# Query loads in whole-row lines, with part of the turned queries moved between partition groups by ScalarE and VectorE, in a pooled attention kernel with a routed feed-forward layer

## The chip, the cores and the metric

The kernel runs on one NeuronCore of one Trainium2 chip. The metric is the device time of one execution in microseconds; an execution's time is compared as the median of several runs, and one execution was profiled.

## The reference

Queries, keys and values come as `(8, 8, 1152, 64)` float32: eight batches, eight heads, 1152 rows, 64 features. Neighbouring query rows are averaged in twos, so 576 pooled queries meet 1152 keys. The attention output of a batch, its heads side by side, is `x` with 576 tokens of 512 features. A gate ranks the tokens of each batch; the 128 best go through a two-layer feed-forward network and are added back.

```python
q_pool = q.reshape(B, H, S // 2, 2, D).mean(axis=3)
scores = np.matmul(q_pool, k.transpose(0, 1, 3, 2)) / np.sqrt(D)
attn = softmax(scores)                      # over the 1152 keys
x = np.matmul(attn, v)                      # bridged to (B, 576, 512)
s = np.einsum('bsd,d->bs', x, w_gate)
top = the 128 largest of s[b]
out[b] = x[b]
out[b, top] = x[b, top] + sigmoid(s[b, top]) * (relu(x[b, top] @ w1) @ w2)
```

## The kernel before

**Order.** The class `_Plain` writes every engine's order out by hand: each engine runs its instructions in the order in which `run` issues them. Two heads make a pair (`hp`), four pairs a batch, 32 pairs in all. The 576 pooled queries of a pair are taken in two halves of 288, `s = 0` and `s = 1`, so `run` loops over 64 halves `h`. One half issues, in this order, the loads of a later pair and stores (at `s = 1`), the scores of this half, small copies of sums of an earlier pair, the row sums of this half's exponents (`folded`), work of earlier halves, `prepare_pair` for the next pair (at `s = 0`), and the product with the values for the half before (`weighted`).

**Layout.** Queries and keys have to stand with their features on the partitions: head 0 of the pair on partitions 0 to 63, head 1 on 64 to 127. VectorE's transpose turns blocks of 32x32, each within its own group of 32 partitions. So `load_pair` puts the first 32 features of head 0 on partition group 0, the last 32 on group 1, and head 1 in the same way on groups 2 and 3 (`quarters`). Each line that such a load reads is 32 floats, 128 bytes. `load_pair` issues four loads for `kb` (L742) and four for `qb` (L745) on SP's queue; the values `v_sb` come by L756, outputs leave by L1024, on the same queue.

**Steps of a pair.** `prepare_pair` adds the two query rows of each pooled query on GpSimd (`qp`, L767), and VectorE turns keys into `kT` (L770) and queries into `qT` (L774). `scores` makes nine PSUM tiles per half with 36 matmuls of 64x64 by 288 columns (L869): the features of one head are the contraction, the columns are 288 queries of `qT`. ScalarE takes the exponent of each tile (L876). `folded` adds the exponents up: GpSimd adds two thirds of them (`acc`, L908), VectorE folds the last third and then `acc` (L913, twice) and finishes with a short reduction (L923). `weighted` multiplies the exponents of the half before with the values (L887, 36 matmuls); ScalarE copies the result out of PSUM (`two`, L895), GpSimd adds its halves (L897), VectorE turns it (`avb`, L966). The rest of a pair is the gate product (L976, L1035), the sums spread over the partitions (L938, L944, L953), their reciprocals (L1005) and the division (L1013).

**Routing.** After the fourth pair of a batch the generator `routed` ranks its tokens in pieces that `units("mid")`, `units("sums")` and `units("end")` put between the steps of later halves. On VectorE these are comparisons (L1145, L1154, L1164), searches (L1229) that wait for a line loaded through DRAM (`lines`, L1198), and a transpose of the gathered tokens (L1284). The feed-forward layers run on TensorE (L1437, L1312, L1332) and, for the first six batches, two batches at a time, with sums on VectorE (L1450) and GpSimd (L1403).

**Buffers.** `qb` and `qp` have one buffer each, `kb`, `kT`, `qT` and `v_sb` two. PSUM holds four tiles of two banks, which scores, `weighted` and the feed-forward layers share.

Of the kernel before, what the change touches and what calls it, by code (L numbers as in the profile page):

```python
# [10 lines left out]
P = 128  # L11
BLK = 32

G = 3
F32 = mybir.dt.float32
# [12 lines left out]
def _any_scores(  # L28
# [450 lines left out]
    pairs = [(b, hp) for b in range(B) for hp in range(NPAIR)]  # L479
    in_pair = [(j, t) for j in range(2) for t in range(NF)] + [(0, NF)]  # L480
    upcoming = load_pair(*pairs[0])
    run(prepare_pair(upcoming))
    preparing = iter(())
    routing = iter(())
# [23 lines left out]
    for n, (b, hp) in enumerate(pairs):  # L508
        pair = upcoming
        run(preparing)  # L510
        if hp == 0:
            x = xpool.tile([P, NT, Dm], F32, name="x")
        for i, (j, t) in enumerate(in_pair):
            now = {"pair": pair, "j": j, "t": t, "x": x}
            advance(now)
            if two is not None and two["t"] == NF and two["pair"]["hp"] == NPAIR - 1:
                run(routing)
                routing = routed(two["pair"]["b"], two["x"])
            one, two = now, one
            if i == 0 and n + 1 < len(pairs):  # L520
                upcoming = load_pair(*pairs[n + 1])
                preparing = prepare_pair(upcoming)
            if n == 0 and i == 0:
                load_weights()
            if i >= 3:
                next(preparing, None)
            next(routing, None)
# [7 lines left out]
class _Plain:  # L535
# [199 lines left out]
    def load_pair(self, b, hp):  # L735

        nc = self.nc
        kb = self.load.tile([P, self.KB, BLK], F32, name="kb")
        qb = self.load.tile([P, self.QB, 2, BLK], F32, name="qb", bufs=1)
        for j, ds, rows in self.quarters():  # L740
            of = self.k[b, 2 * hp + j, :, ds]
            nc.sync.dma_start(kb[rows, :, :], of.rearrange("(i n) d -> i n d", i=BLK))  # L742
        for j, ds, rows in self.quarters():
            of = self.q[b, 2 * hp + j, :, ds].rearrange("(i m) d -> i m d", i=BLK)
            nc.sync.dma_start(qb[rows, :, :, :].rearrange("i n r d -> i (n r) d"), of)  # L745
        return {"k": kb, "q": qb, "b": b, "hp": hp}

    def load_values(self, pair):
# [12 lines left out]
    def prepare_pair(self, pair):  # L761

        nc = self.nc
        qp = self.load.tile([P, self.QB, BLK], F32, name="qp", bufs=1)
        kT = pair["kT"] = self.load.tile([P, self.S], F32, name="kT")
        qT = pair["qT"] = self.load.tile([P, self.Sp], F32, name="qT")
        nc.gpsimd.tensor_tensor(  # L767
            out=qp[:, :, :], in0=pair["q"][:, :, 0, :], in1=pair["q"][:, :, 1, :], op=ALU.add
        )
        nc.vector.transpose(  # L770
            kT.rearrange("p (c g i) -> p c g i", c=self.NC, i=BLK),
            pair["k"].rearrange("p (g c) d -> p c g d", c=self.NC),
        )
        nc.vector.transpose(qT[:, :], qp.rearrange("p n d -> p (n d)"))  # L774

    def load_first(self, b, hp):

# [784 lines left out]
    def run(self):  # L1562
        nc = self.nc
        pairs = [(b, hp) for b in range(self.B) for hp in range(self.NPAIR)]
        n_halves = 2 * len(pairs)
        halves = []
        self.routing, self.waiting = [], set()
        upcoming = self.load_first(*pairs[0])
        self.first_constants()
        self.prepare_first(upcoming)  # L1570
        self.constants()
        loaded = self.load_pair(*pairs[1]) if len(pairs) > 1 else None
        self.load_gate()
        weights = self.weight_loads()
        sums = self.weight_sums() if self.paired else iter(())
        for h in range(n_halves):
            n, s = divmod(h, 2)
            if s == 0:
                pair = upcoming
                if pair["hp"] == 0:  # L1580
                    part = self.ffn.tile([P, self.NPAIR, self.QB], F32, name="part")
                pair["part"] = part
            else:
                loaded = None
                if n + 2 < len(pairs):
                    loaded = self.load_pair(*pairs[n + 2])
                if n + 1 < len(pairs):
                    self.load_values(upcoming)
                if n > 1:
                    self.stored(halves[h - 4]["pair"])  # L1590
            if h > 1:
                next(weights, None)

            if 5 < h < 14 or 18 < h < 23:
                for _ in range(2 - s):
                    next(sums, None)
            half = {"pair": pair, "s": s}
            halves.append(half)
            self.scores(half)
            if h > 1:  # L1600

                of = halves[h - 2 - s]["pair"]
                if s == 0:
                    of["groups"] = self.side_by_side(of["sum"].rearrange("p j n -> p (j n)"))
                else:
                    self.spread(of)
            self.units("mid")
            if h > 2:
                self.gated(halves[h - 3])
            self.folded(half)  # L1610
            if h > 2:
                self.scored(halves[h - 3])
            self.units("sums")
            if h > 1:
                self.multiplied(halves[h - 2])
            if h > 1 and s == 0:
                last = halves[h - 1]["pair"]
                last["total"] = self.added(last["groups"])
            if s == 0 and loaded:
                upcoming = loaded  # L1620
                self.prepare_pair(upcoming)
            if h > 0:
                self.weighted(halves[h - 1])
                self.drained(halves[h - 1])
            if h > 2 and s == 1:
                self.normalized(halves[h - 2]["pair"])
            if h > 3 and s == 0:

                self.divided(halves[h - 3]["pair"])
            self.units("end")  # L1630
        for _ in weights:
            pass
        for _ in sums:
            pass

        def pieces(unit, n=None):
            for i, _ in enumerate(unit):
                if i + 1 == n:
                    break


        left = [unit for _, unit, _ in self.routing]
        old = left.pop() if left else iter(())
        older = left.pop() if left else iter(())
        assert not left
        self.gated(halves[-3])
        pieces(old, 1)
        self.weighted(halves[-1])
        self.drained(halves[-1])
        self.multiplied(halves[-2])  # L1650
        self.multiplied(halves[-1])
        self.scored(halves[-3])
        self.gated(halves[-2])
        pieces(older, 1)
        self.normalized(halves[-1]["pair"])
        self.gated(halves[-1])
        self.scored(halves[-1])
        _, new, _ = self.routing.pop()

        pieces(new, 1)  # L1660
        pieces(old, 1)
        for half in (halves[-3], halves[-1]):
            self.divided(half["pair"])
            self.stored(half["pair"])
        pieces(older, 2)
        pieces(new, 1)
        pieces(old, 1)
        pieces(older, 1)
        pieces(new, 3)
        pieces(older, 4)  # L1670
        pieces(old, self.NFC // 2)
        pieces(new, 1)
        low = self.counted()
        pieces(old, self.NFC // 2 + 1)
        pieces(older)
        pieces(new, 2)
        pieces(old)
        count = self.outside(low)
        pieces(new, 10)
        found = nc.values_load(count[0:1, 0:1])  # L1680
        E = mybir.EngineType
        self.tc.mark_branch_hint_location("again", found, [E.PE, E.DVE, E.Pool, E.Activation, E.SP])
        pieces(new)
        return found
# [61 lines left out]
```

## Time and profile before

| | |
|---|---|
| Median of 3 runs | 689.82 us (689.19 to 692.28) |
| The profiled execution | 689.66 us, its span 687.9 us |
| Busy: TensorE, weight load | 678.0 us (99%), 564.4 us (82%) |
| Busy: VectorE, ScalarE, GpSimd | 536.4 us (78%), 457.7 us (67%), 512.9 us (75%) |
| Granted TensorE clock, mean | 0.998 |
| DMA packets | 397059, of them 377232 under 512 bytes; 101.22 MB |
| Query loads `qb` | 124 issues of 144.0 KB, 3.7 us to landing |

The span goes from the first to the last instruction; the execution's own time has a little around it. Busy shares are of the span. A group of instructions is named by its line, engine, operation and tiles (out<-in). The time behind the last bar of a group is idle time of the engine just before it, with what ended it. In a timeline a row gives start, length, engine, line, operation, tiles and count, and in square brackets the idle time before it.

### The profile page before, as it was taken

To read this page: it belongs to the slowest core of one execution; us is meant where nothing else is said; L and a number is where in the kernel's file an instruction comes from. 1 tells how busy PE (TensorE), PEld (TensorE's weight loads), DVE (VectorE), ACT (ScalarE), POOL (GpSimd) and SP (SyncE) were. 2 spreads that over 40 slices of the span, in tenths; PEclk is the share of its full clock that TensorE was granted. 3 is DMA by queue.
4 is the path that set the end of the run, shared out by engine and by line. 5 is a ranking of instruction groups with operands and counts; after the bars stand their busy time and mean duration, and the time that the engine had idled before them with its cause. 6 is when DMAs were issued, how large, how long until landed. Compare 5 with 4: busy or idle time off the path is not lost.

```text
span 687.9 us, 23660 instructions
## 1 busy us (share of the span) xinstructions
PE 678.0 (99%) x9972; PEld 564.4 (82%) x9972; DVE 536.4 (78%) x842; ACT 457.7 (67%) x998; POOL 512.9 (75%) x503
## 2 busy tenths in 40 slices
PE   9999999999999999999999999999999999999996
PEld 6668899989997998786888899777788899867776
DVE  3867888998999796786698977695879989688930
ACT  5677777777777783847777677583877777575220
POOL 4788888798887775867996978483999888569241
PEclk9999999999999999999999999999999999999999
DMA  9888878688779767953878787783777777644311
GB/s 173 158 176 182 209 143 202 130 155 165 138 167 171 159 136 140 229 101 80 227 129 176 135 166 148 139 197 64 158 190 171 140 152 163 118 116 118 81 47 36
DMA packets 397059, 101.22 MB, mean 147 GB/s; under 512 B 377232, under 2 KB 381200, under 8 KB 395664
## 3 DMA queue, kind: packets, MB, share of 16 engines
q1 hardware_dynamic: 395408, 95.13, 67.1%
q0 software_dynamic: 1296, 4.20, 1.9%
q8 instruction: 80, 1.31, 0.8%
q10 hardware_dynamic: 240, 0.30, 0.2%
q14 instruction: 35, 0.29, 0.1%
HBM read 81.97 MB, written 17.62 MB: 145 GB/s over the span
## 4 chain that ended last, share of the span: by engine, by line
PE 83%; DVE 4%; DMA 4%; issue 4%; POOL 3%; ACT 1%; SPq 0%; POOLq 0%; DVEq 0%; ACTq 0%
PE ps L887 36%; PE ps L869 36%; PE ps L1437 8%; DVE fold L913 2%; DMA out_dram<-xe,index 1%; PE ps L1312 1%; POOL acc L908 1%; ACT p L876 1%; DMA v_sb<-in_v_dram 1%; DMA lines<-row_rank 1%; PE ps L616 1%; DMA row_rank<-both 0%; POOL prod L976 0%; POOL s L1403 0%; DVE pick L1164 0%
## 5 line engine op out<-in xcount | busy, mean ns | idle before, releaser
L876 ACT ACTIVATE p<-ps 128x576 f32<-128x576 f32 x576 | 320.4, 699 | 2.4 <-PE ps L869 2.4
L887 PE MATMUL ps<-p,v_sb 64*64 64x288 f32 x4608 | 296.7, 403 | 2.0 <-DMA v_sb<-in_v_dram 2.0
L869 PE MATMUL ps<-qT,kT 64*64 64x288 f32 x4608 | 296.4, 403 | 0.7 <-DVE token L637 0.5
L908 POOL TENSOR_TENSOR acc<-p 128x576 f32<-128x576 f32 x192 | 272.0, 1444 | 26.7 <-ACT p L876 26.1
L887 PEld LDWEIGHTS ps<-p,v_sb 64*64 64x64 f32 x4608 | 233.7, 133 | 49.9 <-ACT p L876 13.3
L869 PEld LDWEIGHTS ps<-qT,kT 64*64 64x64 f32 x4608 | 229.3, 133 | 51.4 <-ACT p L876 4.6
L913 DVE TRANSPOSE_TENSOR_REDUCE fold<-p 128x54 f32<-128x1728 f32 x64 | 126.0, 1968 | 32.8 <-ACT p L876 32.8
L913 DVE TRANSPOSE_TENSOR_REDUCE fold<-acc 128x54 f32<-128x1728 f32 x64 | 124.7, 1948 | 27.3 <-POOL acc L908 27.3
L895 ACT COPY two<-ps 128x576 f32<-128x576 f32 x64 | 40.8, 637 | 139.0 <-PE ps L887 131.6
L897 POOL TENSOR_TENSOR av<-two 128x288 f32<-128x288 f32 x64 | 51.2, 800 | 68.7 <-ACT two L895 65.4
L767 POOL TENSOR_TENSOR qp<-qb 128x576 f32<-128x576 f32 x31 | 43.7, 1409 | 14.0 <-DMA qb<-in_q_dram 12.9
L976 POOL TENSOR_TENSOR prod<-avb,w_gate 128x288 f32<-128x288 f32 x64 | 51.7, 808 | 1.5 <-DVE red L1035 1.3
L966 DVE STREAM_TRANSPOSE avb<-av 128x288 f32<-128x288 f32 x64 | 29.0, 453 | 23.2 <-POOL av L897 22.8
L770 DVE STREAM_TRANSPOSE kT<-kb 128x1152 f32<-128x1152 f32 x31 | 42.1, 1357 | 0.0
L953 ACT ACTIVATE sums<-total,tiny 32x18 f32<-32x18 f32 x124 | 38.2, 308 | 2.3 <-DVE total L944 0.3
L1013 POOL TENSOR_TENSOR x<-avb,rec 128x576 f32<-128x576 f32 x30 | 34.8, 1160 | 0.0
L1164 DVE SCALAR_TENSOR_TENSOR pick<-sc_row,gate_sc,before 128x128 f32<-128x128 f32 (+1 forms) x40 | 31.3, 782 | 1.4
L938 ACT COPY groups<-sum 32x36 f32<-32x36 f32 x124 | 27.3, 220 | 2.4 <-DVE sum L923 0.7
L1035 DVE TENSOR_REDUCE red<-prod 128x9 f32<-128x288 f32 x64 | 27.7, 433 | 0.1
L1445 ACT COPY s<-ps 128x256 f32<-128x256 f32 (+1 forms) x27 | 11.4, 447 | 20.8 <-PE ps L1437 20.8
L774 DVE STREAM_TRANSPOSE qT<-qp 128x576 f32<-128x576 f32 x31 | 22.6, 730 | 2.1 <-POOL qp L767 2.0
L923 DVE TENSOR_REDUCE sum<-fold 128x18 f32<-128x108 f32 x64 | 21.9, 342 | 2.2
(136 smaller groups left out, 481.7 us busy)
## 6 DMA issues: line engine op xcount, KB each, us to landing
kb<-in_k_dram SPq DMA_DIRECT2D x124, 144.0 KB, 4.5
qb<-in_q_dram SPq DMA_DIRECT2D x124, 144.0 KB, 3.7
v_sb<-in_v_dram SPq DMA_DIRECT2D x124, 144.0 KB, 3.5
tw<-tw SPq DMA_DIRECT2D x10, 1024.0 KB, 7.0
out_dram<-x SPq DMA_DIRECT2D x128, 72.0 KB, 3.0
lines<-row_rank SPq DMA_DIRECT2D x7, 640.0 KB, 4.6
w<-in_moe_w_dram SPq DMA_DIRECT2D x8, 512.0 KB, 6.3
tw<-tw SPq DMA_DIRECT2D x8, 512.0 KB, 5.6
```

What stands on the lines that cost most here:

```text
L767: nc.gpsimd.tensor_tensor(out=qp[:, :, :], in0=pair["q"][:, :, 0, :], in1=pair["q"][:, :, 1, :], op=ALU.add)
L770: nc.vector.transpose(kT.rearrange("p (c g i) -> p c g i", c=self.NC, i=BLK), pair["k"].rearrange("p (g c) d -> p c g d", c=self.NC),)
L869: nc.tensor.matmul(sc[keys, j, 0:n], lhsT=pair["kT"][rows, c * P + keys.start : c * P + keys.stop], rhs=pair["qT"][rows, qs], start=True, ...
L876: nc.scalar.activation(p[:, c // G, c % G, :, :], sc[:, :, 0:n], AF.Exp, scale=self.scale)
L887: nc.tensor.matmul(av[j * self.D : (j + 1) * self.D, e, 0:n], lhsT=half["pair"]["v"][keys, j, c, :], rhs=half["p"][keys, c // G, c % G, j, :],
L895: nc.scalar.copy(two[:, :, :], av[:, :, 0:n])
L897: nc.gpsimd.tensor_tensor(out=half["av"][:, :], in0=two[:, 0, :], in1=two[:, 1, :], op=ALU.add)
L908: nc.gpsimd.tensor_tensor(out=acc[:, u, :], in0=units[:, 0, u, :], in1=units[:, 1, u, :], op=ALU.add)
L913: nc.vector.tensor_reduce(fold[:, a, :], of.rearrange("p u (m d) -> p (u m) d", d=BLK), AX.X, ALU.add, apply_transpose=True,)
L953: self.nc.scalar.activation(tot[rows, :], pair["total"][:, j * self.QB : (j + 1) * self.QB], AF.Identity, bias=self.tiny[0:BLK, 0:1],)
L976: self.nc.gpsimd.tensor_tensor(out=pair["prod"][:, ns, :], in0=pair["avb"][:, ns, :], in1=self.w_gate[:, hp : hp + 1, :].broadcast_to([P, ...
L1437: nc.tensor.matmul(args[0], lhsT=args[1], rhs=args[2], start=k == 0, stop=k == n - 1)
```

## The change

`load_pair` no longer splits the queries by features. It reads 18 whole rows of 64 features, which lie one behind the other in DRAM, as one line of 4608 bytes: partition group 0 gets the first half's queries of head 0 (all 64 features), group 1 the second half's, groups 2 and 3 the same for head 1. The GpSimd addition stays, on tiles of another shape.

The turning now takes two transposes in `prepare_pair`, one for each 32 features. Of these, two blocks per head stand where they belong: features 0 to 31 of the first half, and features 32 to 63 of the second half. The two others have to move between partition groups. `copied_across` copies features 0 to 31 of the second half from the upper to the lower group of the head, on ScalarE, one copy per head. `turned_across` then transposes features 32 to 63 of the first half once more from `qp` in the lower group, straight into the upper group, on VectorE, one transpose per head. Both are issued in the second half (`s == 1`) of the pair before the one whose queries they move: the copies after `spread`, the transposes after `folded`, `scored` and `units("sums")`. The first pair of the kernel is loaded in another way (`load_first`) and isn't touched, so 31 pairs are.

```diff
 def load_pair(self, b, hp):
-        qb = self.load.tile([P, self.QB, 2, BLK], F32, name="qb", bufs=1)
+        qb = self.load.tile([P, self.HB, 2, self.D], F32, name="qb", bufs=1)
...
-        for j, ds, rows in self.quarters():
-            of = self.q[b, 2 * hp + j, :, ds].rearrange("(i m) d -> i m d", i=BLK)
-            nc.sync.dma_start(qb[rows, :, :, :].rearrange("i n r d -> i (n r) d"), of)
+        of = self.q[b, 2 * hp : 2 * hp + 2].rearrange("j (i s m) d -> j s i (m d)", i=BLK, s=2)
+        for g in range(P // BLK):
+            rows = slice(g * BLK, (g + 1) * BLK)
+            nc.sync.dma_start(qb[rows, :, :, :].rearrange("i n r d -> i (n r d)"), of[g // 2, g % 2])
...
 def prepare_pair(self, pair):
-        qp = self.load.tile([P, self.QB, BLK], F32, name="qp", bufs=1)
+        qp = pair["turn"] = self.load.tile([P, self.HB, self.D], F32, name="qp", bufs=1)
...
-        nc.vector.transpose(qT[:, :], qp.rearrange("p n d -> p (n d)"))
+        for e in range(2):
+            nc.vector.transpose(qT[:, self.half_of(e)], qp[:, :, e * BLK : (e + 1) * BLK])
+
+    def half_of(self, s):
+        return slice(s * self.HALF, (s + 1) * self.HALF)
+
+    def crossing(self, j):
+        return slice(j * self.D, j * self.D + BLK), slice(j * self.D + BLK, (j + 1) * self.D)
+
+    def copied_across(self, pair):
+        qT = pair["qT"]
+        for j in range(2):
+            low, high = self.crossing(j)
+            self.nc.scalar.copy(qT[low, self.half_of(1)], qT[high, self.half_of(0)])
+
+    def turned_across(self, pair):
+        qp = pair.pop("turn")
+        for j in range(2):
+            low, high = self.crossing(j)
+            self.nc.vector.transpose(pair["qT"][high, self.half_of(0)], qp[low, :, BLK:])
...
 def run(self):
                     self.spread(of)
+            if s == 1 and "turn" in upcoming:
+                self.copied_across(upcoming)
             self.units("mid")
             if h > 2:
                 self.gated(halves[h - 3])
             self.folded(half)
             if h > 2:
                 self.scored(halves[h - 3])
             self.units("sums")
+            if s == 1 and "turn" in upcoming:
+                self.turned_across(upcoming)
             if h > 1:
                 self.multiplied(halves[h - 2])
```

## Prediction

> **What bounds the kernel now.** I read the page first: busy shares, idle time by group, the chain that ended last.
>
> ```profile
> PE 678.0 (99%) x9972; PEld 564.4 (82%) x9972; DVE 536.4 (78%) x842; ACT 457.7 (67%) x998; POOL 512.9 (75%) x503
> PE 83%; DVE 4%; DMA 4%; issue 4%; POOL 3%; ACT 1%; SPq 0%; POOLq 0%; DVEq 0%; ACTq 0%
> L887 PE MATMUL ps<-p,v_sb 64*64 64x288 f32 x4608 | 296.7, 403 | 2.0 <-DMA v_sb<-in_v_dram 2.0
> L869 PE MATMUL ps<-qT,kT 64*64 64x288 f32 x4608 | 296.4, 403 | 0.7 <-DVE token L637 0.5
> ```
>
> TensorE is idle for 9.9 of 687.9 us, and both attention lines together wait 2.7 us. Anything that makes TensorE wait is paid in full; anything that speeds another engine earns at most those few microseconds. So the question is not how much the loads cost but what the added steps put in front of TensorE. For that I read the timeline of one pair, the second half (s = 1) of an early pair and the start of the next pair, engine by engine: TensorE, then ScalarE, then VectorE. Columns: start, length, engine, line, operation, count, idle time before.
>
> ```profile
> 48.42 4.56 PE L869 MATMUL ps<-qT,kT 64*64 64x288 f32 x72
> 52.78 4.59 PE L887 MATMUL ps<-p,v_sb 64*64 64x288 f32 x72
> 57.15 4.59 PE L869 MATMUL ps<-qT,kT 64*64 64x288 f32 x72
> ```
> ```profile
> 49.25 5.00 ACT L876 ACTIVATE p<-ps 128x576 f32<-128x576 f32 x9
> 54.28 1.27 ACT L953 ACTIVATE sums<-total,tiny 32x18 f32<-32x18 f32 x4
> 57.47 0.64 ACT L895 COPY two<-ps 128x576 f32<-128x576 f32 x1 [1.91 <-PE ps L887]
> ```
> ```profile
> 51.31 0.72 DVE L774 STREAM_TRANSPOSE qT<-qp 128x576 f32<-128x576 f32 x1
> ...
> 54.29 1.98 DVE L913 TRANSPOSE_TENSOR_REDUCE fold<-p 128x54 f32<-128x1728 f32 x1 [1.56 <-ACT p L876]
> 56.19 1.93 DVE L913 TRANSPOSE_TENSOR_REDUCE fold<-acc 128x54 f32<-128x1728 f32 x1
> 58.16 0.34 DVE L923 TENSOR_REDUCE sum<-fold 128x18 f32<-128x108 f32 x1
> 59.02 0.48 DVE L966 STREAM_TRANSPOSE avb<-av 128x288 f32<-128x288 f32 x1 [0.52 <-POOL av L897]
> ```
>
> TensorE takes 8.73 us for a half and goes straight from `weighted` (L887) into the next pair's scores at 57.15. VectorE runs later than TensorE: its fold of the half begun at 48.42 has to wait for the ninth exponent (54.25) and its last step ends at 58.50, **1.35 us after the next pair's scores have begun**. Before the change that is harmless, since nothing in the fold is needed by those scores; qT was finished at 52.03.
>
> **The change, part by part.**
>
> *Loads.* The queries of a pair were 4 x 1152 lines of 128 bytes and become 128 lines of 4608 bytes; over 31 pairs 142,848 of 397,059 packets go. On SP four `qb` issues took 4.20 us in this stretch, four `v_sb` issues, with lines of 2304 bytes, 2.43 us: about 1.8 us less per pair on SP's queue. What can that earn? The waits of L887 for `v_sb`, 2.0 us in all; the idle GpSimd time before L767 (12.9 us for `qb`) is off the path. Between 0 and 2.0 us of gain; I take 2.0.
>
> *GpSimd's add* (L767) keeps its 128x576 elements: 1.4 us, unchanged. `qp` is now held until the last transposes; its next writer comes some 6 us later.
>
> *First transposes.* One L774 of 0.72 us becomes two of 128x288; L966 of that shape lasts 0.45 us. About 0.1 us more, in the first half of a pair, some 5 us ahead of need: nothing on the path.
>
> *ScalarE copies*, two of 32x288 per pair, after L953 in the second half. Bounds from 0.22 us (32x36, L938) to 0.64 us (128x576, L895); by length 0.41 each, 0.8 together. They stand in front of L895, which sat idle 1.91 us waiting for TensorE, so even 2 x 0.64 fits. Their own wait, for the first transposes, ends at about 52.1, 3.4 us ahead. Cost nothing; if that cover were gone, 0.8 us a pair.
>
> *The two late transposes* of 32x288 decide. They write qT's upper rows for queries 0 to 287, which are the very columns that the next pair's first scores read. In VectorE's order of instructions in the changed program they stand directly behind the second half's L923 (behind L1284 or L1450 where these follow it) and ahead of L966; TensorE's first two score matmuls of each pair each get a wait for VectorE. So these scores cannot start before VectorE has finished the fold of the half before, and everything is queued behind that wait: 36 score matmuls, the `weighted` after them, the exponents, the next fold. One transpose of this length: between 0.23 us (L1005, VectorE at 128x18) and 0.73 us (L774, double length); the nearest row is L966 with 0.45 us, 0.40 to the next start, so the pair of them takes 0.85. From VectorE's last write to a score matmul took 0.15 us at the start of the program (qT L828 ends 7.02, L869 starts 7.17).
>
> Stall of a plain transition: 1.35 + 0.85 + 0.15 = **2.35 us**. I compared the end of L923 in the second half with the next L869 for all 31 transitions. In ten the lateness is 1.34 to 1.53 us, in eighteen 3.3 to 6.6, once 0.87. In two (near 295 and 462 us) a feed-forward layer of 12.3 us stands on TensorE between the two, and VectorE is in time. So 29 x 2.35 = 68.2 us.
>
> The later transitions are those where ranking work (L1145, L1154, L1164, L1229, L1284) fills VectorE:
>
> ```profile
> 144.49 4.77 PE L869 MATMUL ps<-qT,kT 64*64 64x288 f32 x71
> ```
> ```profile
> 144.53 1.96 DVE L913 TRANSPOSE_TENSOR_REDUCE fold<-p 128x54 f32<-128x1728 f32 x1
> 146.42 1.93 DVE L913 TRANSPOSE_TENSOR_REDUCE fold<-acc 128x54 f32<-128x1728 f32 x1
> 148.38 0.35 DVE L923 TENSOR_REDUCE sum<-fold 128x18 f32<-128x108 f32 x1
> ```
>
> Here VectorE is 4.25 us late. Taken as they stand, with 1.0 us for transposes and hand-over, all 29 would make 120 us. But much of that is backlog from earlier pairs, and each new stall erases it: TensorE restarts just as VectorE finishes. What counts is VectorE's work between two transitions. In the pair ending here it is 19.75 us busy in 20.2, with 1.0 us added and 0.45 waiting for `av` 21.2, against 17.46 + 2.35 = 19.8: 1.4 more than plain, 2.9 more if nothing is erased. I take 2.0 for the four such pairs: 8 us. Six transitions have L1284 (1.2 us) between L923 and the insertion: 1.0 each, 6 us. Two, after the second feed-forward layers, have GpSimd's part of the fold late (3.8 against 1.35): 1.8 each, 3.6 us. The other late ones fall back to plain.
>
> Sum: 68.2 + 8 + 6 + 3.6 - 2.0 = 83.8 us. The profiled execution took 689.66 us, the median is 689.82: **773.5 us**. Ends: transposes of 0.23 us, 0.41 a pair instead of 0.85, and no extra, 773.5 - 29 x 0.44 - 17.6 = 743; transposes of 0.73 us, 0.55 more a pair, 789; backlog fully kept, 689.66 + 120 - 2 = 808.
>
> *A rule against the change.* In this trace a TensorE wait of 2 us (between 210.4 and 212.5) was followed by 66 matmul records in 4.34 us, the normal pace, while the program's first 20 (L616) took 4.64 us, 232 ns each against 113 for the same size in L1437 (112 in 12.70). A slow state exists at the start, then, and 2 us of waiting did not bring it back; a gap of 3 us and more in mid-kernel no row shows. If each of the twelve longer stalls (3.3 to 4.4 us by the terms above) brought it back and cost half of such a 4.64 us, 28 us would come on top, 801 us; I leave them out, since the 2 us row is the nearest.
>
> The Trainium skill, page "TensorE: Matmul & The Clock Gate", section "HAM oscillation — how this bites in real kernels", warns of TensorE gaps above about 3.4 us, after which the clock is halved: by that rule the plain stalls would be safe and part of the longer ones not, and the sum would lie between 773.5 and 801.
>
> **The rivals.**
>
> *VectorE is in time* (not slower). If the transposes ended before the next scores are due, the kernel would be as before, less the `v_sb` waits: 689.66 - 2.0 = 687.7 us. It decides from the point where the fold ends 2.35 us earlier or TensorE's half lasts as much longer. For it: two transitions where the feed-forward layer does that. Against: 29 where TensorE is back to back, and the fold cannot start before the last exponent. Chance 0.05.
>
> *Backlog stays or the clock falls.* Waits for DMA landings inside the ranking keep VectorE late whatever TensorE does, or the long stalls cost half-speed matmuls: 808 to 836 us (808 + 28). For it: `lines` waits of up to 5.0 us on VectorE. Against: SP's shorter queue brings those landings earlier. Chance 0.09.
>
> *Cheap stall.* The transposes are as short as the lower row and the ranked pairs add nothing: 693 to 750 us. Against: 1.35 us of lateness alone make 39 us (729). Chance 0.06.
>
> The forecast, a stall of 2 to 4 us in 29 of 31 transitions, has 0.80.
>
> **Numbers.** Half a percent, 3.4 us, is about what a measurement here can tell from no change. Slower by more: 0.80 + 0.09 + 0.06 = 0.95; the 0.05 of the first rival divides into 0.03 same and 0.02 faster. The range goes from 750, near the lower end, to 808, where the backlog stays.
>
> **What would show it.** Right: TensorE's share falls to about 88%; the wait table names VectorE's qT (the late transposes) before L869, some 29 times, 60 us or more; the timeline shows L923, two transposes, then L869; under 260,000 packets; no `v_sb` wait. Each step wrong: lateness below 1 us in the plain pairs, transposes outside 0.23 to 0.73 us, stalls of equal length in ranked pairs, or a clock below 1.0. The whole is wrong if L869 shows no wait for VectorE.

## The result, and the profile after

The changed kernel takes 806.25 us (median; 804.59 to 808.32, 6 runs), the kernel before, run beside it, 690.22 us: a ratio of 1.165 with a 95% interval of 1.161 to 1.169. The profiled execution took 805.35 us with a span of 803.5 us, 115.6 us more than the span before. The stalls that were forecast are there, but the time is 33 us above the number forecast (773.5). An experiment below shows where they lie: 27 of them in a halved clock of TensorE, which the sum had left out.

From the page after come busy shares, the granted TensorE clock in 40 slices (in tenths of full speed), packets, and the groups of the scores and of the late transposes (in the changed file L869 is L892, L887 is L910, L913 is L936, L923 is L946; L797 is `turned_across`, L790 `copied_across`):

```profile
PE 723.7 (90%) x9972; PEld 567.6 (71%) x9972; DVE 558.7 (70%) x935; ACT 496.0 (62%) x1060; POOL 514.4 (64%) x503
PEclk9999999989899999999889999999999999998999
DMA packets 258180, 101.23 MB, mean 126 GB/s; under 512 B 234384, under 2 KB 238352, under 8 KB 256784
L892 PE MATMUL ps<-qT,kT 64*64 64x288 f32 x4608 | 339.1, 433 | 73.1 <-DVE qT L797 72.5
L797 DVE STREAM_TRANSPOSE qT<-qp 32x288 f32<-32x288 f32 x62 | 29.1, 470 | 1.9
```

The scores waited 0.7 us in the whole kernel before; now they wait 73.1, of it 72.5 for VectorE's late transposes. Every engine's share of the span fell, since the span is 115.6 us longer. The table of waits counts it:

```profile
PE ps L892 <- DVE qT L797: 72.5, 29, 4.1
```

29 times, as forecast: all transitions from one pair to the next but the two with a feed-forward layer in between. The timeline of an early transition, TensorE and then VectorE:

```profile
65.67 5.09 PE L892 MATMUL ps<-qT,kT 64*64 64x288 f32 x72 [1.67 <-DVE qT L797]
70.44 4.69 PE L910 MATMUL ps<-p,v_sb 64*64 64x288 f32 x72
74.85 4.64 PE L892 MATMUL ps<-qT,kT 64*64 64x288 f32 x72
```
```profile
60.91 1.98 DVE L936 TRANSPOSE_TENSOR_REDUCE fold<-p 128x54 f32<-128x1728 f32 x1 [1.55 <-ACT p L899]
62.81 1.94 DVE L936 TRANSPOSE_TENSOR_REDUCE fold<-acc 128x54 f32<-128x1728 f32 x1
64.79 0.33 DVE L946 TENSOR_REDUCE sum<-fold 128x18 f32<-128x108 f32 x1
65.15 0.97 DVE L797 STREAM_TRANSPOSE qT<-qp 32x288 f32<-32x288 f32 x2
```

The first transpose lets the first matmul go at 65.67, 0.05 us after its end; the second matmul needs the second transpose, 0.5 us later, so the stage is 5.09 us long where the next one, without a wait, is 4.64. Wait and lengthening together are about 2.1 us.

The clock row has not only nines. The next rows are stretches of 3.41 us around a longer stall; columns are start and end, their length, busy time and count of TensorE, weight load, VectorE, ScalarE and GpSimd, granted TensorE clock, DMA share and GB/s.

```profile
160.76:164.17 3.41, 3.41 (x61) 3.27 (x57) 3.30 (x13) 3.32 (x9) 3.41 (x4) 1.00 0.97 220
164.17:167.58 3.41, 1.43 (x24) 0.92 (x16) 3.41 (x5) 1.35 (x4) 1.71 (x3) 1.00 0.36 57
167.58:171.00 3.42, 1.76 (x13) 1.10 (x17) 3.29 (x9) 0.00 (x0) 0.01 (x1) 0.50 0.00 0
171.00:174.41 3.41, 3.41 (x32) 1.82 (x28) 0.95 (x7) 2.46 (x4) 0.00 (x0) 0.50 0.11 21
174.41:177.82 3.41, 3.41 (x60) 2.10 (x56) 0.22 (x1) 3.21 (x8) 3.12 (x3) 1.00 0.99 251
```

TensorE is idle for 2.0 us of the second stretch, and the two that follow run at half clock (0.50): the one that is full of work has 32 matmul records instead of 60. Thirteen such half-rate periods of one or two stretches lie in the span ahead of the last work, 61.4 us at clock 0.5, so up to 30.7 us of lost matmul time. Before, the clock was halved only at the last work of the span (from 685.5 us on).

The account of the 115.6 us: 72.5 of waits, 29 x 0.45 = 13.1 of second waits, 30.7 of halved clock, less the 2.0 of `v_sb` waits, which are gone: 114.3. The terms touch (part of a half-rate period is itself waiting, and idle bars are a little short), so the agreement is good to some microseconds only, and the split between waits and clock is told better by the second experiment.

### The profile page after: what moved, and what is told of

Same layout as the page of the kernel before. It is cut to its first block, busy times and chain, and to the rows that moved or that the text cites. A ratio compares the mean times of both kernels' runs of the same rounds, so it can differ in the third digit from the quotient of the medians.

```text
span 803.5 us, 23786 instructions
## 1 busy us (share of the span) xinstructions
PE 723.7 (90%) x9972; PEld 567.6 (71%) x9972; DVE 558.7 (70%) x935; ACT 496.0 (62%) x1060; POOL 514.4 (64%) x503
## 4 chain that ended last, share of the span: by engine, by line
PE 46%; DVE 21%; ACT 15%; POOL 7%; issue 4%; DMA 4%; SPq 1%; POOLq 0%; ACTq 0%; DVEq 0%
PE ps L892 21%; PE ps L910 16%; ACT p L899 13%; DVE fold L936 13%; PE ps L1460 8%; POOL acc L931 4%; DVE qT L797 2%; DMA out_dram<-xe,index 2%; DVE pick L1187 2%; ACT two L918 2%; DVE sum L946 1%; PE ps L1335 1%; DMA kb<-in_k_dram 1%; DVE xeT L1307 1%; DVE pick L1168 1%
## 5 line engine op out<-in xcount | busy, mean ns | idle before, releaser
L892 PE MATMUL ps<-qT,kT 64*64 64x288 f32 x4608 | 339.1, 433 | 73.1 <-DVE qT L797 72.5
L899 ACT ACTIVATE p<-ps 128x576 f32<-128x576 f32 x576 | 325.6, 684 | 105.3 <-PE ps L892 100.1
L892 PEld LDWEIGHTS ps<-qT,kT 64*64 64x64 f32 x4608 | 222.2, 142 | 179.5 <-DVE qT L797 95.4
L910 PE MATMUL ps<-p,v_sb 64*64 64x288 f32 x4608 | 300.7, 403 | 0.0
L910 PEld LDWEIGHTS ps<-p,v_sb 64*64 64x64 f32 x4608 | 245.5, 133 | 35.3 <-ACT p L899 9.8
L936 DVE TRANSPOSE_TENSOR_REDUCE fold<-p 128x54 f32<-128x1728 f32 x64 | 126.5, 1976 | 153.3 <-ACT p L899 152.9
L936 DVE TRANSPOSE_TENSOR_REDUCE fold<-acc 128x54 f32<-128x1728 f32 x64 | 124.5, 1946 | 9.1 <-POOL acc L931 8.6
L797 DVE STREAM_TRANSPOSE qT<-qp 32x288 f32<-32x288 f32 x62 | 29.1, 470 | 1.9
L790 ACT COPY qT<-qT 32x288 f32<-32x288 f32 x62 | 26.6, 429 | 2.8 <-DVE qT L776 1.4
L1187 DVE SCALAR_TENSOR_TENSOR pick<-sc_row,gate_sc,before 128x128 f32<-128x128 f32 (+1 forms) x40 | 24.5, 611 | 1.4
```

The lines of the kernel that those rows point to most:

```text
L797: self.nc.vector.transpose(pair["qT"][high, self.half_of(0)], qp[low, :, BLK:])
L892: nc.tensor.matmul(sc[keys, j, 0:n], lhsT=pair["kT"][rows, c * P + keys.start : c * P + keys.stop], rhs=pair["qT"][rows, qs], start=True, ...
L899: nc.scalar.activation(p[:, c // G, c % G, :, :], sc[:, :, 0:n], AF.Exp, scale=self.scale)
L910: nc.tensor.matmul(av[j * self.D : (j + 1) * self.D, e, 0:n], lhsT=half["pair"]["v"][keys, j, c, :], rhs=half["p"][keys, c // G, c % G, j, :],
L936: nc.vector.tensor_reduce(fold[:, a, :], of.rearrange("p u (m d) -> p (u m) d", d=BLK), AX.X, ALU.add, apply_transpose=True,)
```

## Experiments

The theory: place alone costs; the late transposes stand behind the fold on VectorE, TensorE's next scores wait for them, and the idle time this leaves halves TensorE's clock now and then. Rivals: the added work on VectorE and ScalarE costs by itself; the new loads cost; the part beyond the waits isn't the clock.

**Everything turned in `prepare_pair`.** The late steps go; four more 32x288 transposes stand behind the first two.

```diff
+        for j in range(2):
+            low, high = self.crossing(j)
+            nc.vector.transpose(qT[low, self.half_of(1)], qp[high, :, 0:BLK])
+            nc.vector.transpose(qT[high, self.half_of(0)], qp[low, :, BLK:])
...
-                self.copied_across(upcoming)
...
-                self.turned_across(upcoming)
```

> The new loads stay; the copies on ScalarE and the two late transposes are gone, and four 32x288 transposes per pair behind the two of 128x288 in prepare_pair (first half of the pair) put the blocks where they belong, so the result is complete. Theory (the place of the late transposes makes TensorE wait, and the gaps bring the halved clock): VectorE has 2.1 us more per pair than before, in a half where it is off the path, so no wait of the scores for VectorE above 2 us in all, no half-rate windows, and 686 to 691 us. Rival A (the added VectorE work costs by itself, wherever it stands): 31 x 2.1 = 65 us more than before, about 755. Rival B (the new form of load costs): above 700 with waits of GpSimd's add for the queries.

Measured: 699.35 us, 1.018 of the kernel before beside it (1.014 to 1.022); no half-rate stretch inside the span. The loss of 116 us shrinks to 12 (by the span to 8), with the loads kept and more VectorE work than in the changed kernel. Rivals A and B fall as explanations (GpSimd's add waited 1.8 us in all for the queries, 12.9 before), but my 686 to 691 was wrong too.

```profile
PE 683.7 (98%) x9972; PEld 573.5 (82%) x9972; DVE 601.3 (86%) x997; ACT 459.3 (66%) x998; POOL 511.5 (73%) x503
L896 PE MATMUL ps<-qT,kT 64*64 64x288 f32 x4608 | 301.9, 404 | 5.0 <-DVE qT L780 3.3 <-ACT two L922 0.9 <-DVE token L637 0.5
```

VectorE is busy for 86%. Where ranking fills it, the next pair's transposes (L780) now end after the scores are due, 3.3 us in all. "Off the path" held for plain pairs only. TensorE's busy time is also 5.7 us longer, in halves with ranking; what stretches it there I did not trace.

**The gap filled.** Matmuls of ones that nobody reads stand ahead of a pair's first scores.

```diff
+            if s == 0 and h > 0 and h not in (32, 48):
+                room = self.banks()[:, 0, 0:P]
+                for _ in range(FILL.get(h, 8)):     # 9 to 17 at the long stalls
+                    nc.tensor.matmul(room, lhsT=self.ones[:, :], rhs=self.ones[:, :], start=True, stop=True)
             self.scores(half)
```

> The changed kernel, with matmuls of ones that nobody reads put on TensorE ahead of the first scores of a pair, 8 of 0.23 us in plain transitions and 9 to 17 in those with long stalls, so that TensorE works through the wait of the scores. Theory (some 31 us of the 116 are matmuls at half clock, brought back by the gaps): half-rate time falls from 61 us to under 10, and the time from 806 to 775 to 785, although the transitions wait as long as before. Rival (the rest beyond the stalls is VectorE or ScalarE falling behind, or a slower first stage of the scores): 803 to 815.

Measured: 779.29 us. The clock is halved only at the last work, and 27 us are gone although TensorE does 307 matmuls more and a plain transition lasts as long as before (from the start of one `weighted` to that of the next 11.13 us in both):

```profile
PEclk9999999999999999999999999999999999999999
L893 PE MATMUL ps<-qT,kT 64*64 64x288 f32 x4608 | 307.8, 405 | 2.5 <-DVE qT L798 0.9 <-DVE token L638 0.5
L1626 PE MATMUL ps<-ones 128*128 128x128 f32 x614 | 76.2, 280 | 0.0
```

So the part beyond the waits was the clock, and idleness of TensorE was what halved it. The waits themselves are still there, filled: 76.2 us of ones. This splits the loss of 116 us: about 89 us without the half clock (779.29 against 690.22), and 27 us for the clock.

**Old loads, late transposes.** The kernel before, with two 32x288 transposes repeated in the late place, and no ScalarE copies.

```diff
-        nc.vector.transpose(qT[:, :], qp.rearrange("p n d -> p (n d)"))
+        for s in range(2):
+            nc.vector.transpose(qT[:, self.half_of(s)], qp[:, s * self.HB : (s + 1) * self.HB, :])
...
+    def turned_late(self, pair):
+        qp = pair.pop("turn")
+        for j in range(2):
+            rows = slice(j * self.D + BLK, (j + 1) * self.D)
+            self.nc.vector.transpose(pair["qT"][rows, self.half_of(0)], qp[rows, 0 : self.HB, :])
```

> The kernel before with its 128-byte loads and no copies on ScalarE; its one transpose of queries is split into two of 128x288, and two of 32x288 are repeated from qp in the place of the late ones, writing the same values again, so that the next scores wait for them. Theory (place alone): within 1% of the changed kernel, 798 to 812 us, with about 14 to 18 half-rate periods. Rival (loads or ScalarE copies have a share in the loss): below 780.

Measured: 808.67 us, 1.176 (1.171 to 1.181), with 15 half-rate periods before the last work. The ratio is within about 1% of the changed kernel's 1.165, so these runs show no share of the loads or the copies in the loss:

```profile
PE ps L880 <- DVE qT L785: 76.5, 29, 4.9
```

**Transposes ahead of the fold.** `turned_across` moves up to just before `folded`, `copied_across` to just before `spread`; the diff is these two pairs of lines in `run`.

> The changed kernel with turned_across issued just ahead of folded and copied_across just ahead of spread, all else the same. Theory: in plain pairs the transposes end about 7.8 us after the second half's scores began, ahead of the next scores at 8.73, no stall; in pairs with ranking work ahead of the fold VectorE gets there at 8 to 11 us and stalls of 0.2 to 3.5 us stay in about a dozen transitions, 8 to 16 us in all, with few half-rate windows: 696 to 712 us. Rival (VectorE's added work is what costs): above 740. Rival (ScalarE's copies ahead of spread delay the next exponents): waits of the exponents' banks on TensorE and above 720.

Measured: 694.55 us, 1.010 (1.006 to 1.014), a little below the expected range of 696 to 712: only one stall of note was left (1.8 us) and no half-rate stretch. It is still 1% slower than the kernel before beside it; where these 7 us lie stays open. In a plain pair:

```profile
55.18 0.97 DVE L797 STREAM_TRANSPOSE qT<-qp 32x288 f32<-32x288 f32 x2 [1.97 <-ACT qT L790]
56.18 1.98 DVE L936 TRANSPOSE_TENSOR_REDUCE fold<-p 128x54 f32<-128x1728 f32 x1
58.09 1.94 DVE L936 TRANSPOSE_TENSOR_REDUCE fold<-acc 128x54 f32<-128x1728 f32 x1
```

The transposes are done before the fold begins, and the fold's end, at 60.4, concerns nobody on TensorE. The same number of instructions as in the changed kernel, in another order, is worth 112 us.

**Late, but unread.** The first experiment with the late steps added again, writing to a part of the running pair's `qT` that is read no more.

```diff
-            self.nc.scalar.copy(qT[low, self.half_of(1)], qT[high, self.half_of(0)])
+            self.nc.scalar.copy(dead[low, self.half_of(0)], qT[high, self.half_of(0)])
...
-            self.nc.vector.transpose(pair["qT"][high, self.half_of(0)], qp[low, :, BLK:])
+            self.nc.vector.transpose(dead[high, self.half_of(0)], qp[low, :, BLK:])
```

> e1_all_in_prepare with the late steps put back as a load without a reader: the same two ScalarE copies and two 32x288 VectorE transposes per pair in the same places, but written to a part of the running pair's qT that is read no more. The result is complete. Theory (the wait, not the work, is what costs): no wait of the scores for the late transposes; what is added is VectorE time, 31 x 1.0 us, in a program that has VectorE at 86% already, so 699 to 712 us and no half-rate windows. Rival (the late work costs wherever it is read or not): above 770.

Measured: 715.23 us, 1.034 (1.029 to 1.039), slightly above what I expected, far below the rival's 770. Work in the late place that no one waits for does not bring the loss back. It adds to an overfull VectorE (88%), whose first transposes are then late more often. I had expected no half-rate stretch; there is one of 3.41 us, at 363 us, behind the longest of these waits (3.45 us). The waits in all:

```profile
L896 PE MATMUL ps<-qT,kT 64*64 64x288 f32 x4608 | 307.7, 408 | 11.4 <-DVE qT L780 9.0 <-ACT two L922 1.5 <-DVE token L637 0.5
```

**The blocks swapped.** Two blocks per head have to cross. The changed kernel lets ScalarE, which is early, move the one that is read a half later, and VectorE, which is late, make the one that is read next. Here each takes the other's block.

```diff
-            self.nc.scalar.copy(qT[low, self.half_of(1)], qT[high, self.half_of(0)])
+            self.nc.scalar.copy(qT[high, self.half_of(0)], qT[low, self.half_of(1)])
...
-            self.nc.vector.transpose(pair["qT"][high, self.half_of(0)], qp[low, :, BLK:])
+            self.nc.vector.transpose(pair["qT"][low, self.half_of(1)], qp[high, :, 0:BLK])
```

> The changed kernel with the two crossing blocks swapped between the two means, at the same places and with the same number of instructions: ScalarE copies features 32 to 63 of the first half's queries, which the next scores read, and the late VectorE transposes make features 0 to 31 of the second half's, which are read a half later. Theory: the copies end 8.1 us after the second half's scores began, ahead of the next scores at 8.73; the late transposes are due only 8.7 us after they end; so no stalls in plain pairs, small ones where ranking holds VectorE's first transposes and with them the copies; no half-rate windows; the v_sb waits of 2.9 us are gone: 686 to 696 us. Rival (the added instructions or the loads cost by themselves): above 720.

Measured: 689.5 us, 0.9965 (0.9944 to 0.9986) of the kernel before beside it. TensorE, ScalarE and VectorE in a plain pair:

```profile
57.60 4.59 PE L892 MATMUL ps<-qT,kT 64*64 64x288 f32 x72
```
```profile
56.03 0.88 ACT L790 COPY qT<-qT 32x288 f32<-32x288 f32 x2
```
```profile
58.99 0.97 DVE L797 STREAM_TRANSPOSE qT<-qp 32x288 f32<-32x288 f32 x2
```

The copies end at 56.91, and the next scores begin at 57.60 without a wait; the transposes end at 59.96, 2.4 us after those scores began, so they are as late as in the changed kernel, but nothing asks for them before 66.3. No `v_sb` wait is left (the page of the kernel before has 2.0 us of them, not the 2.9 of the expectation):

```profile
L892 PE MATMUL ps<-qT,kT 64*64 64x288 f32 x4608 | 297.8, 404 | 2.0 <-ACT two L918 0.7 <-ACT qT L790 0.6 <-DVE token L637 0.5
L910 PE MATMUL ps<-p,v_sb 64*64 64x288 f32 x4608 | 294.8, 403 | 0.0
```

So the new loads can be had at no cost, and this version is the only one whose ratio lies below 1. Its gain of 0.35% is below the half percent named in the prediction, and the kernel before, measured three times beside these versions, had medians of 690.22, 687.21 and 692.56 us, which differ by more; as a gain I would not lean on it.

**Swapped, copies first.** The same, with the copies ahead of `spread`.

> e6_swapped_blocks with the ScalarE copies ahead of spread, so that they end 1.3 us earlier. Theory: 685 to 692 us, at or a little below the kernel before, which has 2.9 us of v_sb waits that these loads take away; if the loads bring nothing, 690 or above. Rival (the copies ahead of spread hold the reciprocals' sums and the stores): waits of VectorE for the sums, 695 and above.

Measured: 692.97 us, 1.001 (0.999 to 1.003): no difference from the kernel before, and above what I expected. It is 3.5 us slower than the version above, with the 12 runs of the one all above the 12 of the other. Moved up, the copies meet VectorE's first transposes before these are ready where VectorE is late (10.9 us of ScalarE waits, against 3.5 in the version above), and two `weighted` copies behind them then hold the scores for 1.0 us each. That is about half of the 3.5 us; the rest stays open.

## Why the prediction came out as it did

**Right: the place and the count.** 29 of 31 transitions stall, each where the scores wait for L797. Lateness of the fold 1.40 us in the shortest case (forecast 1.35), two transposes 0.97 (0.85), hand-over 0.05 (0.15): 2.4 us in place of 2.35, and by so much (2.35 to 2.56 us) a plain pair with no half-rate period lasts longer than before. (The idle bars of TensorE show 2.1 with the second wait, since they begin at the modelled end of the last matmul.) The nearest row, L966 with 0.45, was close to the 0.47 measured.

**Right: backlog is erased.** Five transitions that were 3.3 to 6.6 us late before stall like plain ones, 1.8 to 1.9 us. The four with most ranking wait 3.6 us, 1.9 more than plain (forecast 2.0), the six with L1284 2.4 to 2.8, about 1.0 more (1.0), the two behind feed-forward layers 4.1, 2.4 more (1.8). Not foreseen: the first transition (3.3) and the last (3.7). Waits and second waits make 85.6 us, the forecast stalls 85.8; that these agree so closely is luck, since the bars are some 0.3 us short in each of 29 stalls. The run with the gaps filled is the better measure: 89 us above the kernel before, where the sum had 83.8. So of the 33 us that the sum fell short, about 5 lie in the stalls and 27 in the clock.

**Right: ScalarE's copies cost nothing here**, 0.43 us each (0.41 forecast), and the `v_sb` waits went.

**Wrong: the halved clock, left out of the sum.** It was priced at 28 us (801 in all) and measured at up to 30.7; filling the gaps gave back 27. That the price was so near is partly luck: it stood for the twelve longer stalls, but only eight of these were followed by a half-rate period, and the other five periods followed four plain stalls (1.7 to 1.8 us) and the last one (3.7). The step that failed is "I leave them out, since the 2 us row is the nearest". That row was misread. In the kernel before:

```profile
211.32 0.70 PE L887 MATMUL ps<-p,v_sb 64*64 64x288 f32 x4 [0.91 <-DMA v_sb<-in_v_dram]
212.50 0.72 PE L887 MATMUL ps<-p,v_sb 64*64 64x288 f32 x8 [0.47 <-DMA v_sb<-in_v_dram]
```

TensorE was idle for 0.91 and 0.47 us, 1.4 together, with 0.70 us of work between. It was no evidence that 2 us of idle time are safe; and by the 3.41 us grid of the last section it fell into two stretches, with 0.60 and 0.78 us. The rival that named a falling clock, with a chance of 0.09, was right in that part, and a clock below 1.0, one of the prediction's own signs of a wrong step, is what the profile shows (0.961 on average). That the time still fell inside the range is luck: the upper end of 808 stood for kept backlog, which did not occur, and the half clock took up the room; two of the six runs, at 808.2 and 808.3 us, lie just beyond it.

The Trainium skill's rule in "TensorE: Matmul & The Clock Gate" ("HAM oscillation — how this bites in real kernels") was right that gaps bring the half clock, and not on their size: it warns of gaps above about 3.4 us. Here four stalls of 1.7 to 1.8 us were followed by half clock, and one of 3.63 us (to 650.6 us) was not.

## What to carry to other kernels

Where one engine is busy for 99%, an added step costs by where its result stands in the order of the engine that makes it, against the moment the full engine asks for it, far more than by its length: here the same number of instructions took 806, 695 or 690 us by their order and by which engine did which block. Put the result that is needed first on the engine that is early, and leave to the late engine what is needed later: swapping two blocks was worth 117 us. Count idle time of TensorE twice when some 1.7 us or more of it can fall into one 3.41 us stretch, as here: once for the wait, once for the clock.

## What the runs showed of the hardware that I had not expected

The granted clock changes on a grid of 3.41 us: all half-rate periods of the changed kernel ahead of its last work last 3.41 or 6.83 us, and the stretches at full clock between them are whole multiples too (17.07, 20.48 and 58.03 us are 5, 6 and 17 times as long). I added up TensorE's idle time in each stretch of that grid, for stretches at full clock. In the changed kernel, its last work left out, all eight with 2.0 us of idle time or more were followed by one at half clock, none with 1.66 or less, and between these some were and some were not (1.85, 1.79, 1.79, 1.68 and 1.68 were; 1.92, 1.89, 1.86 and seven more weren't). In the kernel of old loads and late transposes all eleven of 2.0 us or more were. In the run with the late steps unread, of two stretches one behind the other that with 1.96 us was not and that with 1.72 was. So it is idle time within a stretch, about half of it or more, and not the length of a gap, that goes with the halving, and whether a stall does it depends on how it falls on the grid. The stall of 3.63 us that did not halve the clock shows this: it lies across two stretches (columns as above), with 1.89 and 1.74 us of idle time.

```profile
645.47:648.88 3.41, 1.52 (x27) 1.01 (x18) 3.41 (x5) 1.43 (x4) 1.70 (x3) 1.00 0.43 62
648.88:652.30 3.42, 1.68 (x22) 1.00 (x26) 3.29 (x9) 0.33 (x1) 0.10 (x1) 1.00 0.00 0
```

What decides between 1.7 and 2.0 us stays open; in the last experiment 1.5 us between the small transposes on TensorE at the program's start was enough, so what the matmuls are may count too. Idle time here goes by the records, in which the ends of matmuls are modelled.
